# Splitting the last 128-column store of a pruned matmul over two queues, with five late tiles stored in halves

## The chip, the core and the metric

The kernel runs on one core of one Trainium2 chip. The metric is the device time of one execution in microseconds, the median of several runs. Beside it stands one profiled execution, from which all rows of the profile come.

## The reference

The kernel prunes a weight matrix to 2:4 sparsity and multiplies. Of every four consecutive rows of `w`, in each column, the two of largest magnitude are kept (all that reach the second largest), the others become zero; then `x` times the pruned matrix, plus a bias. All arrays are bf16: `x` is 16 x 512 x 1024, `w` 1024 x 1024, `b` 1024.

```python
def reference(x, w, b):
    B, S, D = x.shape
    N, M = 2, 4
    G = D // M
    wg = w.reshape(G, M, D)
    mag = jnp.abs(wg)
    order = jnp.argsort(mag, 1)
    thr = jnp.take_along_axis(mag, order[:, M - N:M - N + 1, :], 1)
    mask = (mag >= thr).astype(w.dtype)
    wp = (wg * mask).reshape(D, D)
    return jnp.einsum("bsd,df->bsf", x, wp) + b
```

## The kernel before

The 16 x 512 tokens are 64 tiles of 128 tokens (`NT` = 64, tiles 0 to 63). A tile's output is 128 rows (the partitions of a tile in on-chip memory) by 1024 columns of bf16, 256 KB.

The first part of the kernel, up to some 40 us, loads `w`, prunes it piece by piece on VectorE and begins the first twelve tiles on TensorE while pieces become ready. It follows orders of instructions for each engine that are written out by hand (the dictionary `order`). The change does not touch this part.

From then on the kernel is a loop over `batches` of tiles (4, then six times 8). SyncE's queue loads a whole batch of `x`, transposed, ahead of its use (`load_batch`). For each tile but the last, 16 matmuls of 128x128 by 128x512 run into two banks of PSUM, one for each half of the columns (`nat`, L242). For each half VectorE then adds the bias and writes the sum as bf16 into the tile's output buffer `o`, one of ten (`evac`, L437). The buffer is stored to DRAM. Tiles before the last `LATE` are stored whole, as one transfer from ScalarE's queue after the second half. The last `LATE` tiles other than tile 63 are stored as two transfers of 512 columns, each from ScalarE's queue after its own half. Before the change `LATE` is 6, so tiles 58 to 62 go out in halves.

Tile 63 is worked off in four groups of columns, 512, 256, 128 and 128, each with its own 8 matmuls, bias add and store. The stores alternate between the queues: 512 from SyncE's, 256 from ScalarE's, 128 from SyncE's, the last 128 from ScalarE's.

All transfers are issued through `issue` (L98), which puts the instruction in program order behind the last one on the same engine, so the profile gives all of them this line. `store` calls `issue` on a range of columns of all 128 rows, and `rows(t)` is the tile's part of the output in DRAM. A transfer waits for the bias add that wrote its columns, and for an earlier transfer that used the same one of eight completion semaphores. When the program ends (L521, the exit of the block that holds the kernel), SyncE waits for all open transfers, and then the engines shake hands and stop.

Of the kernel before, what the change touches and what calls it, by code (L numbers as in the profile page):

```python
# [11 lines left out]
def kernel(  # L12
# [8 lines left out]
    P = 128  # L21
# [7 lines left out]
    Dout = w.shape[1]  # L29
# [13 lines left out]
    STG = 8  # L43
    SOLO = 6
    GROUPS = ((0, 3), (3, 6), (6, 7))
    LATE = 6
    sizes = (4, 8, 8, 8, 8, 8, 8)
    batches = []
    t0 = NPK + LEAD
# [17 lines left out]
    def seq(eng, inst):  # L67
        if eng in tails:
            tc.add_manual_dep(inst.ins, tails[eng].ins.name, NOSYNC, reason="program order")
        tails[eng] = inst  # L70
        return inst
# [24 lines left out]
    def issue(eng, out_, in_):  # L96
        q = nc.sync if eng == "sp" else nc.scalar
        return seq(eng, q.dma_start(out_, in_))  # L98
# [141 lines left out]
    def nat(xt, ps, c0, c1, k0=0, k1=KT, first=0, last=KT - 1, koff=0):  # L240
        for kt in range(k0, k1):
            pe(nc.tensor.matmul(ps, lhsT=xt[:, kt - koff, :], rhs=wp_nat[:, kt, c0:c1],  # L242
                                start=(kt == first), stop=(kt == last)))
# [170 lines left out]
    def load_batch(bi):  # L414
        if bi < len(batches):
            tb, nb = batches[bi]
            xnat.update(load_nat(tb, tb + nb))
# [17 lines left out]
    def evac(o, ps, c0, c1, add=None):  # L435
        if add is None:
            dve(nc.vector.tensor_tensor(o[:, c0:c1], ps, bias_sb[:, c0:c1], op=Alu.add))  # L437
        else:
            dve(nc.vector.tensor_tensor(o[:, c0:c1].rearrange("p (n c) -> p n c", n=2),  # L439
                                        ps.rearrange("p (n c) -> p n c", n=2), add, op=Alu.add))  # L440

    def rows(t):
        return of[t * P:(t + 1) * P, :]

    def store(eng, t, o, c0=0, c1=Dout):
        issue(eng, rows(t)[:, c0:c1], o[:, c0:c1])
# [25 lines left out]
    for bi, (tb, nb) in enumerate(batches):  # L472
        if bi:
            load_batch(bi + 1)
        for j in range(nb):
            t = tb + j
            xt = xnat[t]
            o = outp.tile([P, Dout], bf16, name="o")
            if t == NT - 1:
                for n, (c0, c1) in enumerate(((0, FH), (FH, FH + CW), (FH + CW, Dout - P), (Dout - P, Dout))):  # L480
                    ps = psum_o.tile([P, FH], fp32, name="ps")
                    nat(xt, ps[:, :c1 - c0], c0, c1)
                    evac(o, ps[:, :c1 - c0], c0, c1)
                    store("act" if n % 2 else "sp", t, o, c0, c1)
            else:
                pss = [psum_o.tile([P, FH], fp32, name="ps") for _ in range(2)]
                for kt in range(KT):
                    for h in range(2):
                        nat(xt, pss[h][:], h * FH, (h + 1) * FH, kt, kt + 1)
                for h in range(2):  # L490
                    evac(o, pss[h][:], h * FH, (h + 1) * FH)
                    if t >= NT - LATE:
                        store("act", t, o, h * FH, (h + 1) * FH)
                if t < NT - LATE:
                    store("act", t, o)
# [30 lines left out]
```

## Time and profile before

| | us |
|---|---|
| median of 3 runs | 232.59 |
| lowest and highest run | 232.45 and 233.13 |
| the profiled execution | 232.89 |
| its span, first to last instruction | 231.1 |
| TensorE busy in it | 226.6 |
| granted TensorE clock, mean | 1.000 |

A row of the timeline gives the start, the duration, the engine with its line and operation, what is written and read, and how many instructions are merged in it. PE is TensorE, DVE VectorE, ACT ScalarE, SP SyncE; a q behind the name means an instruction of the engine's queue, such as the issue of a transfer, which is not counted as busy time. The time to landing of a transfer runs from the start of its issue to its last completion signal. The packets of transfers from SyncE's queue are listed as q1, those from ScalarE's as q10; both run on the same 16 DMA engines.

### The profile page before, as it was taken

The page shows a single profiled execution, that of the slowest core. Times are in us where ns is not written, and L with a number is a line of the kernel's source. Part 1 is how long each engine was busy: PE and PEld are TensorE (multiplying, and loading weights), DVE is VectorE, ACT ScalarE, POOL GpSimd, SP SyncE. Part 2 cuts the span into 40 slices and gives each one's busy share as a digit, 9 for nine tenths or more (in the row PEclk, how much of TensorE's full clock was granted, in tenths as well). Part 3 has the DMA queues.
Part 4 walks back from the last instruction along what each step waited for, and adds up shares of the span by engine and source line. Part 5 has one row for each costly group of instructions (what it writes and reads, how often), then busy time and mean ns, then how long its engine had stood idle before and what let it go on. Part 6 is the DMA issues. An engine that isn't in the chain of part 4 may idle for free.

```text
span 231.1 us, 2851 instructions
## 1 busy us (share of the span) xinstructions
PE 226.6 (98%) x1142; PEld 110.9 (48%) x1162; DVE 107.9 (47%) x200; ACT 14.0 (6%) x27; POOL 17.6 (8%) x15
## 2 busy tenths in 40 slices
PE   8999999999999999999999999999999999999995
PEld 5986444444444444444444444444444444444443
DVE  3999877844424424424424424423423423433434
ACT  2874100000000000000000000000000000000000
POOL 1000199700000000000000000000000000000000
PEclk9999999999999999999999999999999999999999
DMA  6999999997399422991259821693128932122122
GB/s 203 276 197 280 164 217 223 297 320 252 124 206 232 155 91 72 237 281 64 75 116 252 222 94 71 162 298 134 65 91 198 273 122 83 54 91 91 53 86 91
DMA packets 79308, 38.19 MB, mean 165 GB/s; under 512 B 64192, under 2 KB 71744, under 8 KB 79296
## 3 DMA queue, kind: packets, MB, share of 16 engines
q1 hardware_dynamic: 68384, 20.75, 43.6%
q10 hardware_dynamic: 10912, 17.27, 20.9%
q8 instruction: 9, 0.15, 0.3%
q14 instruction: 3, 0.02, 0.0%
HBM read 3.28 MB, written 16.78 MB: 87 GB/s over the span
## 4 chain that ended last, share of the span: by engine, by line
PE 98%; issue 0%; DVE 0%
PE ps L242 88%; PE ps L229 5%; PE tp L242 2%; PE ps L138 2%; PE tp L193 1%; PE ps L193 0%; DVE o L437 0%
## 5 line engine op out<-in xcount | busy, mean ns | idle before, releaser
L242 PE MATMUL ps<-wp_nat,xb 128*128 128x512 bf16 (+1 forms) x831 | 178.9, 375 | 0.9
L242 PEld LDWEIGHTS <-xb 128*128 128x128 bf16 x848 | 82.2, 98 | 97.7
L437 DVE TENSOR_TENSOR o<-ps,bias_sb 128x512 bf16<-128x512 f32 (+1 forms) x112 | 71.6, 677 | 113.7 <-PE ps L242 111.4
L433 POOL TENSOR_TENSOR st<-st,bias_sb 128x1024 f32<-128x1024 f32 x8 | 16.7, 2142 | 0.0
L242 PE MATMUL ps<-wp_nat,xlead 128*128 128x512 bf16 x63 | 14.7, 379 | 0.1
L242 PEld LDWEIGHTS <-xlead 128*128 128x128 bf16 x88 | 8.6, 98 | 10.2
L229 PE MATMUL ps<-wp,xt 128*128 128x256 bf16 (+1 forms) x130 | 12.8, 258 | 0.0
L439 DVE TENSOR_TENSOR o<-ps,st 128x512 bf16<-128x512 f32 x16 | 11.1, 691 | 2.8 <-PE ps L242 2.2
L229 PEld LDWEIGHTS <-xt 128*128 128x128 bf16 x130 | 10.9, 98 | 1.1
L242 PE MATMUL ps<-wp_nat,xlow 128*128 128x512 bf16 x47 | 10.6, 379 | 0.1
L264 ACT COPY st<-ps 128x512 f32<-128x512 f32 x14 | 7.4, 600 | 3.2 <-PE ps L229 3.1
L242 PEld LDWEIGHTS <-xlow 128*128 128x128 bf16 x48 | 4.7, 98 | 5.7
L159 DVE TENSOR_TENSOR mag<-mag,hi 128x256 bf16<-128x256 bf16 (+2 forms) x15 | 6.1, 435 | 0.1
L159 DVE TENSOR_TENSOR wp<-w_sb,mag 128x256 bf16<-128x256 bf16 (+2 forms) x15 | 6.1, 435 | 0.1
L242 PE MATMUL tp<-wp_nat,xlead 128*128 128x512 bf16 x23 | 5.8, 380 | 0.0
L138 PE MATMUL ps<-const-bfloat16-1.0 128*128 128x128 bf16 (+1 forms) x20 | 4.2, 408 | 0.8 <-PEq L510 0.8
L169 DVE TENSOR_SCALAR mag<-w_sb 128x512 uint16<-128x512 uint16 (+2 forms) x5 | 2.3, 473 | 3.5 <-DMA w_sb<-in_w_dram 3.5
L138 PEld LDWEIGHTS <-const-bfloat16-1.0 128*128 128x128 bf16 x20 | 2.3, 146 | 2.4 <-issue 2.4
L159 DVE TENSOR_TENSOR hi<-mag 128x512 bf16<-128x512 bf16 (+2 forms) x7 | 3.2, 458 | 0.1
L159 DVE TENSOR_TENSOR lo<-mag 128x512 bf16<-128x512 bf16 (+1 forms) x6 | 3.1, 509 | 0.0
L193 PEld LDWEIGHTS <-x 128*128 128x128 bf16 x28 | 2.3, 124 | 0.3 <-DMA x<-in_x_dram 0.2
L422 POOL COPY pruned<-wp 128x1 bf16<-128x1 bf16 x1 | 0.2, 187 | 26.7 <-DVE wp L159 26.7
(18 smaller groups left out, 18.8 us busy)
## 6 DMA issues: line engine op xcount, KB each, us to landing
out_dram<-o ACTq DMA_DIRECT2D x58, 256.0 KB, 2.4
wp_nat<-wp SPq DMA_DIRECT2D x14, 128.0 KB, 3.2
out_dram<-o ACTq DMA_DIRECT2D x10, 128.0 KB, 1.7
w_sb<-in_w_dram SPq DMA_DIRECT2D x2, 512.0 KB, 5.5
w_sb<-in_w_dram SPq DMA_DIRECT2D x3, 256.0 KB, 5.1
x<-in_x_dram SPq DMA_DIRECT2D x2, 256.0 KB, 4.3
x<-in_x_dram ACTq DMA_DIRECT2D x1, 256.0 KB, 4.0
bias_sb<-in_b_dram SPq DMA_DIRECT2D x1, 256.0 KB, 4.7
```

Source lines behind the costliest of these rows:

```text
L138: pe(nc.tensor.matmul(warm_ps[:, :rep * P], lhsT=nc.const_aps.tensor(1.0, [P, P], bf16), rhs=nc.const_aps.tensor(1.0, [P, rep * P], bf16), ...
L159: dve(nc.vector.tensor_tensor(out, a, b_, op=op))
L169: dve(nc.vector.tensor_single_scalar(mag.bitcast(u16), w_.bitcast(u16), 0x7FFF, op=Alu.bitwise_and))
L193: pe(nc.tensor.transpose(tp[:, m, :], xg[:, m, :], ident[:]))
L229: pe(nc.tensor.matmul(ps[:, c0 + d:c1 + d], lhsT=xpk[t][:, m, :], rhs=wp[:, g, m, c0:c1], start=(new and m == ms.start), stop=(left[key] = ...
L242: pe(nc.tensor.matmul(ps, lhsT=xt[:, kt - koff, :], rhs=wp_nat[:, kt, c0:c1], start=(kt == first), stop=(kt == last)))
L264: act(nc.scalar.copy(staged[(q, h)][:, at, :, :].rearrange("p t c -> p (t c)"), ps_open.pop(key)[:]))
L422: pool(nc.gpsimd.tensor_copy(out=pruned[:], in_=wp[:, 1, 3, Dout - 1:]))
L433: pool(nc.gpsimd.tensor_tensor(st[:], st[:], bias.to_broadcast([P, 2, 2, CW]), op=Alu.add))
L437: dve(nc.vector.tensor_tensor(o[:, c0:c1], ps, bias_sb[:, c0:c1], op=Alu.add))
L439: dve(nc.vector.tensor_tensor(o[:, c0:c1].rearrange("p (n c) -> p n c", n=2), ps.rearrange("p (n c) -> p n c", n=2), add, op=Alu.add))
```

## The change

`LATE` becomes 5, so that tiles 59 to 62 are stored in halves and tile 58 whole (with the divided tile 63 these are five late tiles). In tile 63 the first three stores stay as they are. The store of the last 128 columns, 32 KB from all 128 rows on ScalarE's queue, becomes two transfers of 16 KB: rows 0 to 63 from ScalarE's queue, and rows 64 to 127 from SyncE's. Both wait for the same bias add. The number of transfers in the whole program stays the same.

```diff
@@ -43,7 +43,7 @@
-    LATE = 6
+    LATE = 5
@@ -481,7 +481,11 @@
                     ps = psum_o.tile([P, FH], fp32, name="ps")
                     nat(xt, ps[:, :c1 - c0], c0, c1)
                     evac(o, ps[:, :c1 - c0], c0, c1)
-                    store("act" if n % 2 else "sp", t, o, c0, c1)
+                    if c1 < Dout:
+                        store("act" if n % 2 else "sp", t, o, c0, c1)
+                    else:
+                        issue("act", rows(t)[:P // 2, c0:c1], o[:P // 2, c0:c1])
+                        issue("sp", rows(t)[P // 2:, c0:c1], o[P // 2:, c0:c1])
```

## The prediction

> **What bounds the kernel now.** I read the page first (shares and chain), then the chain for the last ten microseconds, then the timeline, the stores and the packets after the last matmul, because the change touches only code that runs for the last six of 64 token tiles. The page's heading, busy shares and chain:
>
> ```profile
> span 231.1 us, 2851 instructions
> ...
> PE 226.6 (98%) x1142; PEld 110.9 (48%) x1162; DVE 107.9 (47%) x200; ACT 14.0 (6%) x27; POOL 17.6 (8%) x15
> ...
> PE 98%; issue 0%; DVE 0%
> ```
>
> TensorE is busy for 226.6 of 231.1 us and carries 98% of the chain. The change removes no matmul, so up to the last matmul nothing can be gained, and what is left to move is the tail. Its rows: the end of the chain, the timeline from 228 us on, and the timeline between 228.7 and 229 us, which separates the last ScalarE issue from the one before it.
>
> ```profile
> 226.28 2.16 PE ps L242 x25
> 228.44 0.02 issue
> 228.46 0.29 DVE o L437
> ```
>
> ```profile
> 228.03 1.10 ACTq L98 DMA_DIRECT2D out_dram<-o  x2
> 228.34 0.34 SPq L98 DMA_DIRECT2D out_dram<-o  x1
> ...
> 228.79 0.34 ACTq L98 DMA_DIRECT2D out_dram<-o  x1
> ```
>
> The last matmul ends at 228.44, VectorE adds the bias to the last 128 columns until 228.75, and ScalarE's queue starts issuing their store at 228.79. The chain stops there, although the span goes on to 231.1. What fills those 2.3 us is seen in the store's own rows (first two lines), in SyncE's waits after 228 us (third line) and in the rows of the closing code after 230.1 us (last two):
>
> ```profile
> L98 ACTq DMA_DIRECT2D out_dram<-o x1: 339/339/339, 228.8 to 228.8; - x1
> DMA to landing us min/median/max: 1.4/1.4/1.4
> ...
> SPq L521 <- DMA out_dram<-o: 1.3, 4, 0.4
> ...
> L521 SPq EVENT_SEMAPHORE x3: 17/17/28, 230.2 to 231.0; - x3
> L521 SPq DRAIN x3: 7/7/13, 230.3 to 230.6; - x3
> ```
>
> From the start of its issue to its landing the last store takes 1.4 us: 228.79 + 1.4 = 230.2. At 230.2 SyncE, which at the end of the program (L521) waits for every open store, is released, and the closing handshake takes 231.1 - 230.2 = 0.9 us. So the end is set by matmul, bias add (0.29), issue and landing (1.4), handshake (0.9), one after another; only the 1.4 is touched. Inside it:
>
> ```profile
> 229.40:229.60 0.20, 0.00 (x0) 0.00 (x0) 0.00 (x0) 0.00 (x0) 0.00 (x0) 1.00 0.03 5
> 229.60:229.80 0.20, 0.00 (x0) 0.00 (x0) 0.00 (x0) 0.00 (x0) 0.00 (x0) 1.00 0.65 142
> 229.80:230.00 0.20, 0.00 (x0) 0.00 (x0) 0.00 (x0) 0.00 (x0) 0.00 (x0) 1.00 0.12 22
> ```
>
> These are stretches of 0.2 us; the last two numbers are the mean busy share of the 16 DMA engines and the rate. The store's packets begin at about 229.6, 0.8 after the issue began, and keep an engine busy for 0.2 x 0.65 + 0.2 x 0.12 = 0.15 us on average. The rest, some 0.4 us, is the way to the semaphore. So of 1.4 us only the issue (0.34) and the packets (0.15) can depend on the number of rows.
>
> **The change, part by part.** First the late tiles. With LATE at 5, tile 58 no longer stores its halves apart; one store of 256 KB goes out after its second bias add. Its bias adds and the landing times of the three sizes concerned:
>
> ```profile
> 210.94 1.29 DVE L437 TENSOR_TENSOR o<-ps,bias_sb 128x512 bf16<-128x512 f32 x2 [2.17 <-PE ps L242]
> ...
> out_dram<-o ACTq DMA_DIRECT2D x58, 256.0 KB, 2.4
> ...
> out_dram<-o ACTq DMA_DIRECT2D x10, 128.0 KB, 1.7
> ```
>
> Issued at 210.94 + 1.29 = 212.2, it lands at about 212.2 + 2.4 = 214.6 instead of 212.3 + 1.7 = 214.0, more than 16 us before the end. Those 16 us of matmuls hide it; nobody reuses its output buffer, as ten buffers serve the pool and only five tiles follow. Were the cover gone, it would cost 0.6. One ScalarE issue of 0.34 goes, on an engine that only issues stores there. Cost: nothing.
>
> Second, the last store. Removed: one issue of 128 rows on ScalarE's queue. Added: one of rows 0-63 there, and one of rows 64-127 on SyncE's queue, both released by the same bias add. Is SyncE free? Its previous store is issued from 228.34 for 0.34, to 228.68, 0.11 before 228.79. At the start of the kernel it issues back to back:
>
> ```profile
> 0.73 0.45 SPq L98 DMA_DIRECT2D w_sb<-in_w_dram  x1
> 0.74 0.50 ACTq L98 DMA_DIRECT2D w_sb<-in_w_dram  x1
> ...
> 1.24 0.45 SPq L98 DMA_DIRECT2D x<-in_x_dram  x1
> ```
>
> The first issue ends at 1.18 and the next begins at 1.24, a gap of 0.06, within the 0.11. So both halves start at about 228.79. Queued behind SyncE's new issue are its final waits; they begin 0.34 later than now, but the stores they wait for land later still, so nothing is lost.
>
> What one half costs alone: the transfers of 0.73 and 0.74 have 256 pieces each and take 0.45 and 0.50 to issue, against 0.34 for the 128 rows of a store. That is 0.11 for 128 pieces from the SyncE row; 64 rows fewer would save 0.06 and a half's issue would take 0.28 (an estimate; the trace has no store of 64 rows, so the bounds are no saving and half, 0.17). Its packets take half of 0.15, so 0.08 less. A half alone would land 0.06 + 0.08 = 0.14 earlier, after 1.26.
>
> What two at once cost is the term that decides. The trace has two pairs of equal transfers issued from the two queues within 0.01 us: the rows above, and two copies of 128 KB at 22.4 us. For the first, the packets by queue in three consecutive stretches, 1.5 to 1.84, 1.84 to 2.28 and 2.28 to 2.30 us (q1 is SyncE's, q10 ScalarE's):
>
> ```profile
> q1 hardware_dynamic: 1, 0.00, 0.5%
> ...
> q1 hardware_dynamic: 85, 0.04, 40.7%
> ...
> q1 hardware_dynamic: 7, 0.00, 62.8%
> q10 hardware_dynamic: 1, 0.00, 8.4%
> ```
>
> SyncE's packets begin before 1.84, ScalarE's after 2.28: at least 0.44 later, about one issue (0.45), although the instructions began 0.01 apart. The landing times of this pair (two lines), and of the pair at 22.4 with its issue rows:
>
> ```profile
> w_sb<-in_w_dram SPq DMA_DIRECT2D x1, 128.0 KB, 2.7
> w_sb<-in_w_dram ACTq DMA_DIRECT2D x1, 128.0 KB, 2.9
> ```
>
> ```profile
> L98 SPq DMA_DIRECT2D wp_nat<-wp x1: 554/554/554, 22.4 to 22.4; - x1
> L98 ACTq DMA_DIRECT2D wp_nat<-wp x1: 637/637/637, 22.4 to 22.4; - x1
> ...
> DMA to landing us min/median/max: 2.6/2.9/3.1
> ```
>
> The second of a pair lands 0.2 and 0.5 us after the first. The Trainium skill (Perfetto Trace Analysis, DMA Instruction — HWDGE) says the block that makes the descriptors is locked by one issuing queue at a time; by that page the second half would follow a whole issue behind the first. The trace agrees as to packets (0.44 apart) but not as to instruction records (0.50 and 0.64, not doubled).
>
> Scaled to halves: the packets of the second half start one half-issue, 0.28, behind the first's, which start 0.06 earlier than the whole store's do now: +0.22. They take 0.08 less: +0.14. The lower bound has no offset and a half's full saving, -0.14; the upper has no saving in the issue and the larger of the two offsets in landing, 0.5 - 0.08 = +0.42. I take +0.15, near the row of 0.2 rather than that of 0.5, because packets and issue here are shorter than in either pair. The sum against the profiled execution: 232.89 + 0.15 = 233.04, its span becoming 231.1 + 0.15 = 231.2, with 1.8 around it as before. The profiled execution lies 0.30 above the median of the runs, which carries the same tail: 232.59 + 0.15 = 232.74. The bounds are 232.59 - 0.14 = 232.45 and 232.59 + 0.42 = 233.01.
>
> **The rivals.** Side by side. The queues don't queue up behind each other for a store this small; both halves' packets start 0.06 earlier and share the 16 engines for the same 0.15. Time: 232.59 - 0.06 = 232.53 (232.45 at best). For it: the issue records of both pairs overlap, and q1 and q10 packets mix in the last stretch. Against it: the 0.44. The Trainium skill (DMA: Bandwidth & Descriptors, Rules for kernel authors) says of two transfers to disjoint partition halves "Don't bother — they serialize", since both spread over the same 16 engines; by that page alone the gain would be at most the sequencer's share. The trace agrees that 0.15 of engine time is not halved by a second queue.
>
> Slower: an issue is held up by the other queue. All stores of ScalarE's queue:
>
> ```profile
> L98 ACTq DMA_DIRECT2D out_dram<-o x70: 338/338/958, 37.5 to 228.8; - x70
> ```
>
> One of them took 0.96 instead of 0.34. If the second half's issue met that, 0.62 comes on top of 0.15: 232.59 + 0.77 = 233.36. This matters from the point at which the two together pass 0.70 us, 0.3% of 232.59 and about what a measurement of this kernel can tell from no change: an issue of 0.34 + 0.55 = 0.89 or more. For it: the two queues do disturb each other (0.64 against 0.55). Against it: the median of 70 is the minimum, and the pairs added 0.05 and 0.08.
>
> The store isn't the bound. Had the closing code some other thing to wait for, nothing would move: 232.59. Against it stand SyncE's four waits for stores; for it, that the chain on the page ends at VectorE.
>
> **How the numbers follow.** Second half behind the first, +0.05 to +0.42: 0.60. Side by side: 0.25. Held up: 0.10. Not the bound: 0.05. Only the third leaves the band of 0.70 by itself. The three runs of before spread over 232.45 to 233.13, 0.3%, so drift can carry a small loss over the line, and a small gain much more rarely: slower 0.14, faster 0.03, within 0.83. The likeliest case gives 232.74, its own range 232.64 to 233.01. The range runs from a little under the lower bound, 232.40, to 233.25, beyond the upper bound and the highest run of before but short of the third case.
>
> **What would show it.** In the changed profile: two issues of 64 rows near 228.79, one on each queue, with records of 0.17 to 0.34 (nearest 0.28); the packets of one queue starting some 0.3 after the other's; the later half landing 1.5 to 1.6 after its issue; the span 231.1 to 231.5; one 256 KB store of tile 58 near 212.3. Packets of both queues starting together and landings of 1.3 would mean side by side; an issue above 0.89 the slower case; a last landing that moves while the closing waits don't would mean that the store was never the bound. I'd be wrong altogether if anything ahead of 228.4 shifted, since no row there depends on these lines.

## The result, and the profile after

| | us |
|---|---|
| kernel before, median of 12 runs (lowest to highest) | 232.53 (232.25 to 233.13) |
| changed kernel, median of 12 runs | 233.31 (232.94 to 233.66) |
| ratio, 95% interval | 1.0031, 1.0021 to 1.0041 |
| profiled execution of the changed kernel, its span | 232.94, 231.2 |

The change makes the kernel slower by 0.3%, about 0.7 us. The forecast was 232.74 in a range of 232.40 to 233.25, and a loss of more than 0.70 us had a chance of 0.14. The heading, busy time and chain of the changed kernel's page:

```profile
span 231.2 us, 2851 instructions
...
PE 225.8 (98%) x1142; PEld 110.1 (48%) x1162; DVE 107.8 (47%) x200; ACT 13.9 (6%) x27; POOL 17.6 (8%) x15
...
PE 96%; DMA 1%; issue 1%; SPq 0%; DVE 0%
```

The span is only 0.1 longer than before's 231.1, so the whole-span numbers hide the loss. The start of the chain says why, first in the kernel before, then (three lines) in the changed kernel, followed by the end of its chain:

```profile
0.77 4.21 PE ps L138 x20
4.99 1.02 PE tp L193 x8
```

```profile
1.25 3.39 DMA x<-in_x_dram
4.63 0.04 issue
4.68 0.64 PE tp L193 x8
...
227.88 0.29 DVE o L437
```

The first tiles of `x` landed 0.3 us sooner in this execution, and the first eight transposes took 0.64 us instead of 1.02. That put the program ahead: its last bias add ends at 228.17, against 228.75. No line of the change runs there; single executions differ like this (over all profiled executions here the last bias add ends between 228.2 and 229.6). What can be compared is the stretch from the end of the last bias add to the end of the span. It was 2.32 us and is now 2.98 (unrounded times of the trace, here and below): 0.66 more, which is the loss of the runs within their interval.

A single stretch isn't exact either. Three of the experiments below (e3, e8 and e9) end with the same stores as the kernel before, and their stretches are 2.41, 2.46 and 2.63. Most of the spread lies behind the last landing. From the last bias add to the last landing these four executions take 1.48 to 1.54 us; the changed kernel takes 2.08, so 0.54 to 0.60 more. The stretch in the timeline, then the two issues with their times to landing:

```profile
228.20 0.56 SPq L98 DMA_DIRECT2D out_dram<-o  x1
228.20 0.59 ACTq L98 DMA_DIRECT2D out_dram<-o  x1
```

```profile
L98 SPq DMA_DIRECT2D out_dram<-o x1: 564/564/564, 228.2 to 228.2; - x1
L98 ACTq DMA_DIRECT2D out_dram<-o x1: 592/592/592, 228.2 to 228.2; - x1
...
DMA to landing us min/median/max: 1.8/1.9/2.0
```

Both queues start at once, 0.03 after the bias add, as forecast. But each half takes longer to issue than the whole store did (0.56 and 0.59 against 0.34), and the later half lands 2.0 us after its issue began instead of 1.4. The packets in two consecutive stretches, 229.40 to 229.67 and 229.67 to 229.70 us:

```profile
q1 hardware_dynamic: 80, 0.02, 33.8%
...
q10 hardware_dynamic: 7, 0.00, 34.4%
```

None ran from 228.9 to 229.4. SyncE's 80 packets come first; ScalarE's begin 0.27 us after the first of SyncE's. SyncE's first packet comes 1.21 us after the issue began, where the whole store's came after 0.84. The closing code after 230.2 us, then (last line) that of e3 after 229.9 us:

```profile
L525 SPq EVENT_SEMAPHORE  x4: 17/22/28, 230.3 to 231.1; - x4
L525 SPq DRAIN  x3: 7/7/13, 230.4 to 230.7; - x3
...
L521 SPq EVENT_SEMAPHORE  x4: 17/22/28, 229.9 to 230.8; - x4
```

One wait more than before (x3) falls behind the last landing, and it starts 0.06 after the one before it. From the last landing to the end it is 0.90 us, against 0.84. This isn't the split's doing: e3, which has no split, has the same wait and 0.90, e4, which has the split, has three and 0.83, and e9, with an unchanged end, has seven and 1.09.

So the 0.66 between these two executions consists of: first half's packets 0.36 later, second half's 0.27 after those, packets and signal 0.03 shorter, closing 0.06 longer.

### The profile page after: what moved, and what is told of

The parts are those of the page before. It is cut to its first block, busy times and chain, and to the rows that moved or that the text cites. A ratio compares the mean times of both kernels' runs of the same rounds, so it can differ in the third digit from the quotient of the medians.

```text
span 231.2 us, 2851 instructions
## 1 busy us (share of the span) xinstructions
PE 225.8 (98%) x1142; PEld 110.1 (48%) x1162; DVE 107.8 (47%) x200; ACT 13.9 (6%) x27; POOL 17.6 (8%) x15
## 4 chain that ended last, share of the span: by engine, by line
PE 96%; DMA 1%; issue 1%; SPq 0%; DVE 0%
PE ps L242 88%; PE ps L229 5%; PE tp L242 2%; DMA x<-in_x_dram 1%; PE tp L193 0%; PE ps L193 0%; SPq L98 0%; DVE o L437 0%
## 5 line engine op out<-in xcount | busy, mean ns | idle before, releaser
L138 PE MATMUL ps<-const-bfloat16-1.0 128*128 128x128 bf16 (+1 forms) x20 | 3.7, 359 | 0.8 <-PEq L514 0.8
L159 DVE TENSOR_TENSOR hi<-hi,lo 128x128 bf16<-128x128 bf16 (+2 forms) x8 | 2.1, 287 | 0.1
```

Of the source, the lines that this page charges most:

```text
L138: pe(nc.tensor.matmul(warm_ps[:, :rep * P], lhsT=nc.const_aps.tensor(1.0, [P, P], bf16), rhs=nc.const_aps.tensor(1.0, [P, rep * P], bf16), ...
L159: dve(nc.vector.tensor_tensor(out, a, b_, op=op))
```

## The experiments

Two theories stood first. A: two queues that issue at the same instant slow each other. B: a transfer of 64 rows is slow to issue by itself. The second median of each pair is that of the kernel before, run again beside the experiment; the ratio and its interval are those on record, which aren't the quotient of the two medians.

**Both halves from one queue** (e1).

```diff
                         issue("act", rows(t)[:P // 2, c0:c1], o[:P // 2, c0:c1])
-                        issue("sp", rows(t)[P // 2:, c0:c1], o[P // 2:, c0:c1])
+                        issue("act", rows(t)[P // 2:, c0:c1], o[P // 2:, c0:c1])
```

> As the changed kernel, but both halves of the last store are issued from ScalarE's queue, one after the other. Theory A (two queues that issue at the same instant slow each other): each half's issue takes 0.28 us (0.17 to 0.34) instead of 0.56 and 0.59, the second half lands some 0.3 later than the whole store did, the stretch from the end of the last bias add to the end of the span is 2.6 us (2.32 in the kernel before, 2.98 in the changed one), and the time is 0.2 to 0.35 us above the kernel before. Theory B (a store of 64 rows is slow to issue by itself, on any queue): the records stay at about 0.57 each, the two in a row end 1.2 after the bias add, the stretch is 3.2 us or more, and the time 0.9 us or more above the kernel before.

Median 233.62 against 232.58, ratio 1.0038 (1.0025 to 1.0052). The end of its chain and the two issues:

```profile
229.30 0.29 DVE o L437
```

```profile
L98 ACTq DMA_DIRECT2D out_dram<-o x2: 563/582/602, 229.6 to 230.2; - x2
DMA to landing us min/median/max: 1.8/1.8/1.8
```

With a span of 232.9, the stretch is 232.9 - 229.59 = 3.3 us. The first half had no other issue beside it and still took 0.563. A has fallen as the cause of the long issue. B's numbers hold; its loss of 0.9 or more is 1.04 by the medians and 0.88 by the ratio.

**The same columns split by columns** (e2): 64 columns of all 128 rows from each queue.

```diff
-                        issue("act", rows(t)[:P // 2, c0:c1], o[:P // 2, c0:c1])
-                        issue("sp", rows(t)[P // 2:, c0:c1], o[P // 2:, c0:c1])
+                        cm = (c0 + c1) // 2
+                        issue("act", rows(t)[:, c0:cm], o[:, c0:cm])
+                        issue("sp", rows(t)[:, cm:c1], o[:, cm:c1])
```

> As the changed kernel, but the last 128 columns are split by columns: 64 columns of all 128 rows from each queue at the same instant. Theory A: two issues at once are slow whatever their shape, and as each has 128 rows the records are 0.57 to 0.7 us and the stretch from the last bias add to the end is 3.0 us or longer (2.32 before), the time 0.7 to 1.0 us above the kernel before. Theory B: without 64-row transfers the records are back at 0.34, the stretch at 2.3 to 2.5, the time within 0.2 us of the kernel before.

Median 232.75 against 232.58, ratio 1.0010 (0.9993 to 1.0026).

```profile
L98 SPq DMA_DIRECT2D out_dram<-o x1: 377/377/377, 228.5 to 228.5; - x1
L98 ACTq DMA_DIRECT2D out_dram<-o x1: 367/367/367, 228.5 to 228.5; - x1
...
DMA to landing us min/median/max: 1.6/1.6/1.7
```

The issues are 0.03 to 0.04 us longer than the 0.34 of a lone store, not 0.25, and their packets begin 0.03 apart. That is B again in issue and time. The stretch, 2.59, is a little above B's 2.5, but within the 2.32 to 2.63 of the unchanged ends; up to the last landing it is 1.76, 0.22 to 0.28 more than theirs.

**Each part of the change alone** (e3 and e4): `LATE = 5` in the kernel before, and `LATE = 6` in the changed kernel.

> The kernel before with LATE at 5 alone: tile 58 stored whole, the last 128 columns in one store from ScalarE's queue. Both theories: no change, 0.0 within 0.15 us, the last issue 0.34, the stretch from the last bias add to the end 2.3 us. If the whole loss or a part of it came from tile 58, it would show here as up to 0.7 us.

Median 232.47 against 232.58, ratio 0.9990 (0.9978 to 1.0002): tile 58 costs nothing.

> The split of the last store alone, with LATE left at 6. Both theories: the whole loss, 0.6 to 0.8 us above the kernel before, two records of about 0.57 us at the same instant, the stretch from the last bias add to the end 2.9 to 3.0 us. If the eight completion semaphores mattered (one transfer more now shifts which earlier transfer each waits for), the issues of the halves would begin later than 0.05 us after the bias add.

Median 233.17 against 232.58, ratio 1.0018 (1.0005 to 1.0031).

```profile
L98 SPq DMA_DIRECT2D out_dram<-o x1: 554/554/554, 228.8 to 228.8; - x1
L98 ACTq DMA_DIRECT2D out_dram<-o x1: 586/586/586, 228.8 to 228.8; - x1
```

The split alone has the slow issues, a stretch of 2.92 us (2.09 of it up to the last landing, against 2.08 in the changed kernel) and a loss of 0.59 by the medians and 0.42 by the ratio. The intervals of the split alone and of the whole change overlap. Both issues begin 0.03 after the bias add, so the shifted completion semaphores don't hold up the issues.

**Issue time by rows** (e8, e9). Other stores in tiles 55 to 61, long before the end, from ScalarE's queue. Here is e8's code without the branch for tile 61, which goes out in four transfers of 64 rows by 512 columns; e9 has other cuts and its tile 61 in rows 32-95, 0-31, 96-127.

```diff
+                cut = {56: (0, 64, 128), 57: (0, 32, 64, 96, 128), 58: (0, 96, 128), 59: (0, 112, 128), 60: (0, 120, 128)}
+                if t in cut:
+                    for ra, rb in zip(cut[t], cut[t][1:]):
+                        issue("act", rows(t)[ra:rb, :], o[ra:rb, :])
...
```

> The kernel before with other stores in tiles 56 to 61, well ahead of the end and all from ScalarE's queue, to read the issue time of a transfer by its rows: tile 56 in two of 64 rows, 57 in four of 32, 58 in 96 + 32, 59 in 112 + 16, 60 in 120 + 8 (all of 2 KB rows), 61 in four of 64 rows by 512 columns. Theory B1 (only a full 128 rows is quick to issue): every one takes 0.5 us or more, against 0.34 for 128 rows. Theory B2 (the issue time falls as rows are added, with 128 as the end of a slope): 120, 112 and 96 lie between 0.34 and 0.5, 64 at 0.56, 32 and fewer above 0.6. Theory B3 (what counts is the number of descriptors of each DMA engine, rising with rows): 64 rows 0.56 only for 256-byte rows; with 2 KB rows 0.34 or less. The end of the program is that of the kernel before: time within 0.3 us of it.

The first issues of tiles 56, 57, 58, 59 and 60, which are 64, 32, 96, 112 and 120 rows:

```profile
L98 ACTq DMA_DIRECT2D out_dram<-o x1: 566/566/566, 205.5 to 205.5; - x1
...
L98 ACTq DMA_DIRECT2D out_dram<-o x1: 346/346/346, 208.9 to 208.9; - x1
...
L98 ACTq DMA_DIRECT2D out_dram<-o x1: 323/323/323, 212.4 to 212.4; - x1
...
L98 ACTq DMA_DIRECT2D out_dram<-o x1: 322/322/322, 215.8 to 215.8; - x1
...
L98 ACTq DMA_DIRECT2D out_dram<-o x1: 573/573/573, 219.3 to 219.3; - x1
```

All three theories miss: there is no slope. 32, 96 and 112 rows are as quick as 128; 64 rows are slow with 2 KB rows too. The four transfers of 64 rows by 512 columns took 0.47 to 0.61. Its one time, 233.13, decides nothing, as runs of the kernel before on the same chip reached 233.12.

The 120 rows can't be read from this. They were issued for tile 60, and at the same place a store of all 128 rows, the second half of tile 60, was slow in three other traces: 0.57 in the kernel before and 0.60 in e3 (the two lines), 0.47 in e4. In the six other traces that leave tile 60 in two halves it took 0.34.

```profile
L98 ACTq DMA_DIRECT2D out_dram<-o x1: 567/567/567, 219.2 to 219.2; - x1
...
L98 ACTq DMA_DIRECT2D out_dram<-o x1: 600/600/600, 218.8 to 218.8; - x1
```

What holds up an issue there isn't known. At the places where 64 rows were read in e8 and e9, the stores of 128 rows in the other traces took 0.34. The 8 rows right behind the 120 took 0.29, where an issue right behind one of 64 rows took 0.52 or more.

> A second reading of issue time by rows in another order, in tiles 55 to 61, all from ScalarE's queue with rows of 2 KB: 96 + 32, 16 + 112, 48 + 80, 80 + 48, 64 + 64, 32 + 96, and rows 32-95 followed by 0-31 and 96-127. If the count of rows sets it: first issues of 96, 16 and 32 rows take 0.30 to 0.36 us, 64 again 0.56 wherever it starts, also from row 32. If the first partition or the order of issue sets it: 64 rows from row 32 is quick, or 96 and 32 take other times than 0.32 and 0.35. 48 and 80 were not tried: if 64 alone is slow they take 0.36 or less, if even counts per DMA engine are slow, or odd ones, one of 48, 80 and 112 joins it.

The first issues of 96, 16, 48 and 80 rows took 0.348, 0.321, 0.322 and 0.322 us. 64 rows from row 0, 32 from row 0, and 64 from row 32:

```profile
L98 ACTq DMA_DIRECT2D out_dram<-o x1: 561/561/561, 216.0 to 216.0; - x1
...
L98 ACTq DMA_DIRECT2D out_dram<-o x1: 326/326/326, 219.4 to 219.4; - x1
...
L98 ACTq DMA_DIRECT2D out_dram<-o x1: 581/581/581, 222.9 to 222.9; - x1
```

For 64 rows the count sets it, not the first row and not the place in the program. A second issue close behind a quick one took 0.43 to 0.44, and 0.60 behind one of 64 rows, even for 32 rows. The one time of e9 is 233.41.

**Pieces or rows** (e6).

```diff
+                        pc = lambda v: v.rearrange("p (a s c) -> p s a c", a=2, s=2)
+                        dr, sb = pc(rows(t)[:, c0:c1]), pc(o[:, c0:c1])
+                        issue("act", dr[:P // 2, 0], sb[:P // 2, 0])
+                        issue("sp", dr[P // 2:, 0], sb[P // 2:, 0])
+                        issue("act", dr[:, 1], sb[:, 1])
```

> As the changed kernel, but the last 128 columns are stored in blocks of 32 columns, so that every row has two pieces of 64 bytes in a transfer: rows 0-63 of blocks 0 and 2 from ScalarE's queue, rows 64-127 of them from SyncE's at the same instant, then all 128 rows of blocks 1 and 3 from ScalarE's. It parts the number of pieces from the number of rows. If pieces count: 64 rows by 2 pieces are 128 pieces and take 0.34 to 0.4 us to issue, 128 rows by 2 take 0.45. If rows count: 64 rows by 2 pieces take 0.56 or more, 128 by 2 stay below 0.5.

```profile
L98 SPq DMA_DIRECT2D out_dram<-o x1: 695/695/695, 228.2 to 228.2; - x1
L98 ACTq DMA_DIRECT2D out_dram<-o x1: 727/727/727, 228.2 to 228.2; - x1
...
L98 ACTq DMA_DIRECT2D out_dram<-o x1: 832/832/832, 229.0 to 229.0; - x1
```

128 pieces from 64 rows are slower still, so it isn't the number of pieces that 64 rows lack. But 128 rows of two pieces took 0.83, against the expectation for rows; as this issue follows right behind a slow one, e6 doesn't tell whether the second piece or the place in the queue made it so long. The one time of this kernel is 233.76.

**The split at a quick count** (e5), with the theory that was left: 64 is a slow count of rows, and the split as such costs little.

```diff
-                        issue("act", rows(t)[:P // 2, c0:c1], o[:P // 2, c0:c1])
-                        issue("sp", rows(t)[P // 2:, c0:c1], o[P // 2:, c0:c1])
+                        issue("act", rows(t)[:96, c0:c1], o[:96, c0:c1])
+                        issue("sp", rows(t)[96:, c0:c1], o[96:, c0:c1])
```

> As the changed kernel, but the last 128 columns are split at row 96: rows 0-95 from ScalarE's queue, 96-127 from SyncE's, at the same instant. Theory C (64 is a slow count of rows, 96 and 32 are quick ones, and a split as such costs little): issues of 0.32 to 0.4 us, the stretch from the last bias add to the end 2.3 to 2.6 us (2.98 with 64 + 64), the time within 0.3 us of the kernel before. Theory D (two transfers of fewer than 128 rows take turns whatever the count, the second's packets 0.27 us behind the first's): the stretch is 2.6 to 2.8 us and the time 0.3 to 0.5 us above the kernel before. If all fewer than 128 rows were slow at the end of the program: 2.9 or more, as in the changed kernel.

Median 232.60 against 232.46, ratio 1.0004 (0.9993 to 1.0016). The issues and landings, and the packets from 229.21 to 229.24 us:

```profile
L98 SPq DMA_DIRECT2D out_dram<-o x1: 384/384/384, 228.3 to 228.3; - x1
L98 ACTq DMA_DIRECT2D out_dram<-o x1: 378/378/378, 228.3 to 228.3; - x1
...
DMA to landing us min/median/max: 1.4/1.5/1.6
```

```profile
q1 hardware_dynamic: 11, 0.00, 47.7%
q10 hardware_dynamic: 2, 0.00, 7.5%
```

Same bytes, same queues, same instant, cut 32 rows further on, and the loss is gone from the time. Packets of both queues start 0.03 apart; D has fallen with its 0.27. The stretch, 2.53, lies within the 2.32 to 2.63 of the unchanged ends. Up to the last landing it is 1.63, still 0.09 to 0.15 more than theirs, so the split brings nothing either.

**A narrower last group** (e7), to look for something better than both kernels.

```diff
-                for n, (c0, c1) in enumerate(((0, FH), (FH, FH + CW), (FH + CW, Dout - P), (Dout - P, Dout))):
+                for n, (c0, c1) in enumerate(((0, FH), (FH, FH + CW), (FH + CW, Dout - 64), (Dout - 64, Dout))):
```

> The kernel before with tile 63 in groups of 512, 256, 192 and 64 columns instead of 512, 256, 128 and 128, each stored in one transfer of 128 rows. As a transfer of 128 rows takes 0.34 us to issue whatever its width, only the last bias add gets shorter: by the rows for 512, 256 and 128 columns (0.69, 0.42, 0.29 us) 0.23 for 64, a gain of 0.06 us. If eight matmuls of 64 columns take as long as eight of 128 (0.44 us), TensorE ends 0.22 us later and the time is 0.16 us above the kernel before. Between the two: within 0.2 us of the kernel before either way.

Median 232.75 against 232.62, ratio 1.0002 (0.9993 to 1.0011). The end of the groups by form, between 226 and 229 us, and the issues:

```profile
L437 DVE TENSOR_TENSOR o<-ps,bias_sb 128x64 bf16<-128x64 f32 x1 | 0.2, 214 | 0.0
```

```profile
228.46 0.34 SPq L98 DMA_DIRECT2D out_dram<-o  x1
228.60 0.34 ACTq L98 DMA_DIRECT2D out_dram<-o  x1
```

The last bias add took 0.21 instead of 0.29, but the store of the 192 columns before it now starts only 0.14 ahead of the last one, and both land 1.6 after their issue instead of the 1.4 that the last one took before. As VectorE comes to the last bias add straight from the 192 columns, only 0.04 of the 0.08 is left: the last bias add ends 0.29 after the last matmul instead of 0.33. From there to the last landing it is 1.64, 0.10 to 0.16 more than with the unchanged ends, so the gain is lost again; why both stores land later isn't shown. No version tried is shown to beat the kernel before.

## Why the prediction was wrong

- **What bounds the end** was right. Matmuls, bias add, landing, closing handshake stand in that order, and the loss arose between bias add and handshake.
- **Tile 58 at no cost** was right: 0.9990 (0.9978 to 1.0002) when it was changed alone.
- **SyncE free in time** was right: its issue began 0.005 us ahead of ScalarE's.
- **A half's issue at 0.28** is the step that failed. It measured 0.56 and 0.59. The slope came from transfers with two pieces to a row, and I let it run down below 128 rows as if fewer rows could only be cheaper; even my bound was "no saving". So the first half's packets came 0.36 later, not 0.06 earlier. The row that should have been the upper bound stood in my own text: the copies at 22.4 us with issues of 0.55 and 0.64, for as many bytes as a store that takes 0.34. With 0.55 the upper bound would have been 0.21 higher, 233.22 instead of 233.01, and with 0.64 it would have been 233.31.
- **The second half 0.28 behind the first** measured 0.27. The number was met by luck: the rule behind it, one half-issue, gives 0.56 with the measured issue. I took the delay for a property of any two issues at once, and it is absent for 128 + 128 (e2) and 96 + 32 (e5). It was seen with 64 + 64 alone.
- **Packets 0.08 shorter**: 0.03. The 64 packets of a half still spread over 0.23 us, against 0.26 for the 128 of the whole store, and both halves together kept the 16 engines busy for 0.18 us on average, against 0.15.
- **The closing handshake unchanged**: 0.06 longer in this pair of executions, but not because of the split (e3 and e4).
- **The slower rival** had the direction and nearly the size (0.77) by another mechanism. No issue reached its 0.89, and e1 shows the slow issue with no other issue beside it.
- **The side-by-side rival**: in e5 the packets of the two queues do overlap, and still nothing was gained, as the last landing came no earlier.
- **The forecast span**, 231.1 to 231.5, was met by luck: at 231.2 it holds the loss and, against it, the 0.58 us by which this execution was ahead at the last bias add.
- The Trainium skill's advice against two transfers of disjoint partition halves (DMA: Bandwidth & Descriptors, Rules for kernel authors) fits the outcome. Its reason, that they serialize, fits the packets of 64 + 64, 0.27 apart, but not those of 96 + 32, 0.03 apart. Its statement that one queue at a time locks the descriptor block (Perfetto Trace Analysis, DMA Instruction — HWDGE) doesn't show in e2: both issues ran at once, in 0.37 and 0.38.

What stays open is why 64 rows are slow while 16, 32, 48, 80, 96, 112 and 128 aren't. 16, 48, 80 and 112 rows were read once each. The profile shows only the longer record and the later packets. Whether 120 rows are slow stays open too, and loads were not tried.

## What to carry to other kernels

A transfer on the path to the end should be issued with a count of rows whose issue time the trace has shown; less data is not by itself a cheaper issue, and splitting a small one saves nothing where issue and completion, not packets, fill its time. To judge a change at the end of a program, compare the stretch from the last unchanged instruction to the last landing, because the start alone moved this span by 0.6 us, and the closing after the last landing took 0.83 to 1.09 us in the kernel before, e3, e4, e8 and e9. A bound for an operation the trace doesn't have should include the slowest row of its kind, in the direction that seems absurd too.

## What the runs showed of the hardware that I had not expected

A store of 64 rows took 0.55 to 0.61 us to issue, longer than one of 128 rows at 0.34, whether the rows had 256 bytes or 2 KB (0.47 to 0.61 with 1 KB). In the changed kernel its packets start 1.21 us after the issue begins, instead of 0.84. Two quick issues from both queues at the same instant were only 0.03 to 0.06 us longer than such issues alone. Each wait of SyncE that is left behind the last landing lengthened the closing by 0.06 us (0.84 with three such instructions of SyncE behind it, 0.90 with four, 1.09 with seven).
